# Gate-loop attention with a maxout FFN on one core: the attention output computed with features in rows, on four column quarters of the array

## The chip, the cores and the metric

The kernel runs on one core of a Trainium2 chip. The metric is the device time of one execution in microseconds (us), the smaller the better. PE is TensorE's matmuls, PEld its weight loads, DVE VectorE, ACT ScalarE, POOL GpSimd and SP SyncE.

## The reference

```python
# batch 4, heads 8, sequence 768, head dim 48; all float32
for t in range(S):                                   # complex gated recurrence, per head
    new_re = ar * S_re - ai * S_im                   # ar, ai: the normalised gate of token t
    new_im = ar * S_im + ai * S_re
    S_re, S_im = new_re + k_t (x) v_t, new_im
    y[:, :, t] = einsum('bhd,bhde->bhe', q_t, S_re)
x = y.transpose(0, 2, 1, 3).reshape(3072, 384)       # tokens x features
h = max(x @ w1, x @ w2, x @ w3)                      # 384 -> 768
out = h @ w_out                                      # 768 -> 384
```

The kernel turns the recurrence into blocks of 128 tokens (two chunks of 64). Within a chunk, every output is a sum over the chunk's tokens (a 64 x 64 matrix `atm` of scores per head, times V). What came earlier enters through a state G (the decayed query `QG`, times G).

## The kernel before

A group is two blocks. For each block TensorE makes transposes of K and Q (`tp`), decay sums (`mds`, `sfx`, `F`), scores (`A`, `B`), the state update (`dk`), and the output `y`. Between those blocks the FFN of the group before is woven in (`up`: 384 to 768, three weights; `op`: 768 to 384). `cs` is a running sum over tokens for the gates of the next group, and it waits for DVE's `w`. The FFN needs `x` with features in rows, while `y` comes out with tokens in rows, so y is copied out of PSUM, transposed by three PE transposes, and copied again.

```python
    vbs = [const.tile([P, H, 2, D], FP, name="vb%d" % i) for i in range(4)]
...
    def load_v(g):
        if g >= NG:
            return
        for c in range(C):
            x = g * C + c
            T["v", x] = vbs[x % 4]
            for h in range(2):
                nc.sync.dma_start(out=T["v", x][h * L64:(h + 1) * L64, :, h], in_=rows(v, g, c, h * L64, L64))
...
    def state(x):

        s = x % NS
        if s == 0:
            T["G", x] = st.tile([P, H, 2, D], FP, tag="G", name="G")
            nc.gpsimd.memset(T["G", x][0:DD, :, 0], 0.0)
        ps = psS.tile([P, 2, 512], FP, tag="s", name="dk")
        for h in range(H):
            nc.tensor.matmul(out=ps[0:DD, h // HU, h % HU * 96:h % HU * 96 + 96],
                             lhsT=T["Kt", x][:, h].rearrange("p u d -> p (u d)"),
                             rhs=T["v", x][:, h].rearrange("p c d -> p (c d)"), start=True, stop=True)
        dk = ps[0:DD, :, 0:HU * 96].rearrange("p a (b c d) -> p a b c d", b=HU, c=2)
        G = T["G", x]
        for c in range(2 if s < NS - 1 else 1):
            if c == 0:
                new = G[0:DD, :, 1]
            else:
                T["G", x + 1] = st.tile([P, H, 2, D], FP, tag="G", name="G")
                new = T["G", x + 1][0:DD, :, 0]
            add = new.rearrange("p (a b) d -> p a b d", b=HU)
            if s + c == 0:
                nc.vector.tensor_copy(out=add, in_=dk[:, :, :, c])
                continue
            f = T["F", x][0:DD, :, CD + c:CD + c + 1].to_broadcast([DD, H, D])
            nc.vector.tensor_tensor(out=new, in0=G[0:DD, :, c], in1=f, op=OP.mult)
            nc.vector.tensor_tensor(out=add, in0=add, in1=dk[:, :, :, c], op=OP.add)

    def outputs(x):
        atm, V, G, QG = T["atm", x], T["v", x], T["G", x], T["QG", x]
        y = psM.tile([P, DM], FP, tag="mm", padded_shape=[P, 512], name="y")
        for h in range(H):
            for new in (True, False):
                for c in range(2):
                    o = c * L64
                    nc.tensor.matmul(out=y[o:o + L64, h * D:(h + 1) * D],
                                     lhsT=atm[:, h] if new else QG[0:DD, 2 * h + c],
                                     rhs=V[:, h, c] if new else G[0:DD, h, c], start=new, stop=not new)
        T["x", x] = fp2.tile([P, DM], FP, tag="x", name="x")
        nc.scalar.copy(out=T["x", x], in_=y)

    def xt_step(x, xs):
        n = len(xs) * P
        if x == xs[0]:
            T["xT", xs[-1]] = fp2.tile([P, KD, n], FP, tag="xT", padded_shape=[P, KD, TG], name="xT")
        tp = psM.tile([P, KD, P], FP, tag="mm", padded_shape=[P, 4, P], name="tpx")
        for f in range(KD):
            nc.tensor.transpose(out=tp[:, f], in_=T["x", x][:, f * P:(f + 1) * P], identity=ident)
        o = (x - xs[0]) * P
        nc.scalar.copy(out=T["xT", xs[-1]][:, :, o:o + P], in_=tp)
...
    def up_step(xs, fp, i):
        xT, n = T["xT", xs[-1]], len(xs) * P
        ...  # up[f] += ws[i][:, d, f].T @ xT[:, d]: xT has features in rows
...
    def loop_steps(g):
        steps = []
        for x in range(g * C, (g + 1) * C):
            tr, ct, pr = front(x + 1)
            kt = [products(x + 1)[2]] if x + 1 < NX else []
            steps += [call(scores, x, "A"), call(gather, x, "A"), call(scores, x, "B")] + tr[:1]
            steps += [call(gather, x, "B"), call(state, x)] + tr[1:] + ct + pr[:1] + kt
            steps += [call(outputs, x)] + pr[1:2] + [call(xt_step, x, tokens(x))] + pr[2:]
        return steps
```

Of the kernel before, what the change touches and what calls it, by code (L numbers as in the profile page):

```python
# [9 lines left out]
FP = mybir.dt.float32  # L10
# [4 lines left out]
OP = mybir.AluOpType  # L15
# [30 lines left out]
def kernel(  # L46
# [13 lines left out]
    nc = tc.nc  # L60
    B, H, S, D = q.shape
    P = 128
# [26 lines left out]
    nat2 = ctx.enter_context(tc.tile_pool(name="nat2", bufs=2))  # L89
    un1 = ctx.enter_context(tc.tile_pool(name="un1", bufs=1))  # L90
    un2 = ctx.enter_context(tc.tile_pool(name="un2", bufs=2))
    st = ctx.enter_context(tc.tile_pool(name="st", bufs=2))
    fp2 = ctx.enter_context(tc.tile_pool(name="fp2", bufs=2))
    psS = ctx.enter_context(tc.tile_pool(name="psS", bufs=2, space=PSUM))
    psM = ctx.enter_context(tc.tile_pool(name="psM", bufs=4, space=PSUM))
# [49 lines left out]
    masko = const.tile([P, 4, 32], U8, name="masko")  # L145


    vbs = [const.tile([P, H, 2, D], FP, name="vb%d" % i) for i in range(4)]
    atms = [const.tile([P, H, L64], FP, name="atm%d" % i) for i in range(2)]

    def constants_early():
# [26 lines left out]
    def constants_late():  # L178
# [21 lines left out]
        for t in atms:  # L200
            nc.gpsimd.memset(t, 0.0)


    def rows(a, g, c, lo=0, n=P):
        b, s = divmod(g, GB)
        t0 = (s * C + c) * P + lo
        return a[b, :, t0:t0 + n, :].rearrange("h t d -> t h d")
# [15 lines left out]
# [4 lines that stand above are left out]
            x = g * C + c  # L227
            T["v", x] = vbs[x % 4]
            for h in range(2):
                nc.sync.dma_start(out=T["v", x][h * L64:(h + 1) * L64, :, h], in_=rows(v, g, c, h * L64, L64))  # L230

    ws = [const.tile([P, KD, FF], FP, name="w%d" % i) for i in range(3)]
    wo = const.tile([P, KF, DM], FP, name="wo")
# [270 lines left out]
    def state(x):  # L504

        s = x % NS
        if s == 0:
            T["G", x] = st.tile([P, H, 2, D], FP, tag="G", name="G")
            nc.gpsimd.memset(T["G", x][0:DD, :, 0], 0.0)
        ps = psS.tile([P, 2, 512], FP, tag="s", name="dk")  # L510
        for h in range(H):
            nc.tensor.matmul(out=ps[0:DD, h // HU, h % HU * 96:h % HU * 96 + 96],  # L512
                             lhsT=T["Kt", x][:, h].rearrange("p u d -> p (u d)"),
                             rhs=T["v", x][:, h].rearrange("p c d -> p (c d)"), start=True, stop=True)
        dk = ps[0:DD, :, 0:HU * 96].rearrange("p a (b c d) -> p a b c d", b=HU, c=2)
        G = T["G", x]
        for c in range(2 if s < NS - 1 else 1):
            if c == 0:
                new = G[0:DD, :, 1]
            else:  # L520
                T["G", x + 1] = st.tile([P, H, 2, D], FP, tag="G", name="G")
                new = T["G", x + 1][0:DD, :, 0]
            add = new.rearrange("p (a b) d -> p a b d", b=HU)
            if s + c == 0:
                nc.vector.tensor_copy(out=add, in_=dk[:, :, :, c])
                continue
            f = T["F", x][0:DD, :, CD + c:CD + c + 1].to_broadcast([DD, H, D])
            nc.vector.tensor_tensor(out=new, in0=G[0:DD, :, c], in1=f, op=OP.mult)
            nc.vector.tensor_tensor(out=add, in0=add, in1=dk[:, :, :, c], op=OP.add)  # L529

    def outputs(x):
        atm, V, G, QG = T["atm", x], T["v", x], T["G", x], T["QG", x]
        y = psM.tile([P, DM], FP, tag="mm", padded_shape=[P, 512], name="y")
        for h in range(H):
            for new in (True, False):
                for c in range(2):
                    o = c * L64
                    nc.tensor.matmul(out=y[o:o + L64, h * D:(h + 1) * D],  # L538
                                     lhsT=atm[:, h] if new else QG[0:DD, 2 * h + c],
                                     rhs=V[:, h, c] if new else G[0:DD, h, c], start=new, stop=not new)  # L540
        T["x", x] = fp2.tile([P, DM], FP, tag="x", name="x")
        nc.scalar.copy(out=T["x", x], in_=y)


    def xt_step(x, xs):
        n = len(xs) * P
        if x == xs[0]:
            T["xT", xs[-1]] = fp2.tile([P, KD, n], FP, tag="xT", padded_shape=[P, KD, TG], name="xT")
        tp = psM.tile([P, KD, P], FP, tag="mm", padded_shape=[P, 4, P], name="tpx")
        for f in range(KD):  # L550
            nc.tensor.transpose(out=tp[:, f], in_=T["x", x][:, f * P:(f + 1) * P], identity=ident)
        o = (x - xs[0]) * P
        nc.scalar.copy(out=T["xT", xs[-1]][:, :, o:o + P], in_=tp)  # L553

    def up_step(xs, fp, i):
        xT, n = T["xT", xs[-1]], len(xs) * P
# [24 lines left out]
    def call(f, *a):  # L581
        return lambda: f(*a)
# [21 lines left out]
# [4 lines that stand above are left out]
            kt = [products(x + 1)[2]] if x + 1 < NX else []  # L608
            steps += [call(scores, x, "A"), call(gather, x, "A"), call(scores, x, "B")] + tr[:1]
            steps += [call(gather, x, "B"), call(state, x)] + tr[1:] + ct + pr[:1] + kt  # L610
            steps += [call(outputs, x)] + pr[1:2] + [call(xt_step, x, tokens(x))] + pr[2:]
        return steps

    table("natural_log_exp_and_others")
    for t in vbs:
        nc.gpsimd.memset(t, 0.0)
    load(0)
    load_v(0)
# [54 lines left out]
```

## Time and profile before

| what | before |
|---|---|
| median of 3 timed executions | 777.61 us (777.31 to 778.47) |
| the profiled execution | 776.25 us, span 774.3 us, clock 0.969 |
| PE busy in the span | 698.6 us (90%) |
| DVE, ACT busy | 515.8 us (67%), 405.5 us (52%) |
| one group of two blocks, steady | 56.87 us, of which PE busy 56.45 |
| y, 32 matmuls = 64 records, of one block | 2.00 us |
| three transposes of one block, in the chain | 0.33 us |

The prediction shows the lines behind this table. A group in the chain of waits is the distance from one block to the same block two further on. A "record" is what the profile counts as one instruction: a float32 matmul of the code shows as two records, a transpose as one.

### The profile page before, as it was taken

The numbers are of one execution on the slowest core, as the hardware profiler recorded it, in microseconds if no ns is written. First come the engines' busy times: TensorE is split into PE (matmuls) and PEld (weight loads), VectorE is DVE, ScalarE is ACT, GpSimd is POOL, SyncE is SP. The second block draws the span as 40 slices with busy tenths as digits, with TensorE's granted clock in tenths as the row PEclk, the third lists the DMA queues.
The fourth block names the chain that finished last, engine by engine and source line by source line (L and its number), as shares of the span: only waits on it lengthen the run. The fifth ranks groups of instructions, "written<-read, shape, count | busy, mean of one in ns | idle before, by whom it ended". The sixth has DMA issues, their size and how long they took to land.

```text
span 774.3 us, 14595 instructions
## 1 busy us (share of the span) xinstructions
PE 698.6 (90%) x6156; PEld 570.3 (74%) x6156; DVE 515.8 (67%) x706; ACT 405.5 (52%) x677; POOL 115.9 (15%) x124
## 2 busy tenths in 40 slices
PE   1174579999799999999999999999999999999998
PEld 0063378978678778878878878878878878878775
DVE  4899997788764865865855856866766767645211
ACT  6685645667555564664564564564564564412010
POOL 7003100403102202202102112112112013000000
PEclk9987589999899999999999999999999999999999
DMA  9663430050220320410410410410410210000000
GB/s 228 108 175 115 119 82 23 11 103 2 52 62 11 63 52 11 77 38 11 83 40 4 85 40 2 93 31 7 87 32 12 42 32 2 1 21 2 11 11 20
DMA packets 133377, 38.70 MB, mean 50 GB/s; under 512 B 126016, under 2 KB 129088, under 8 KB 133312
## 3 DMA queue, kind: packets, MB, share of 16 engines
q1 hardware_dynamic: 133056, 37.76, 22.0%
q8 instruction: 48, 0.79, 0.4%
q14 instruction: 17, 0.14, 0.1%
q10 hardware_dynamic: 256, 0.01, 0.0%
HBM read 33.03 MB, written 4.72 MB: 49 GB/s over the span
## 4 chain that ended last, share of the span: by engine, by line
PE 70%; DVE 18%; ACT 2%; issue 1%; DVEq 0%; ACTq 0%
PE up L564 30%; PE op L575 12%; PE tp L416 5%; PE dk L512 4%; PE y L538 4%; PE F L433 4%; PE B L476 4%; DVE QB L443 3%; DVE Q L443 3%; PE cs L337 3%; PE A L476 2%; DVE QG L443 2%; DVE KB L443 2%; DVE w L333 1%; DVE w L334 1%; PE sfx L377 1%
## 5 line engine op out<-in xcount | busy, mean ns | idle before, releaser
L564 PE MATMUL up<-xT,w 128*128 128x256 f32 (+1 forms) x1404 | 301.3, 366 | 0.7 <-ACT xT L553 0.7
L564 PEld LDWEIGHTS up<-xT,w 128*128 128x128 f32 x1404 | 246.6, 191 | 38.1 <-issue 1.1
L569 DVE TENSOR_TENSOR hT<-hT,up 128x512 f32<-128x512 f32 (+1 forms) x78 | 50.1, 642 | 87.4 <-PE up L564 85.5
L575 PE MATMUL op<-wo,hT 128*128 128x384 f32 x288 | 98.1, 490 | 0.0
L316 POOL TENSOR_TENSOR ai<-ai,L 128x768 f32<-128x768 f32 x11 | 27.6, 2509 | 394.0 <-ACT L L107 361.5
L575 PEld LDWEIGHTS op<-wo,hT 128*128 128x128 f32 x288 | 52.9, 190 | 32.6
L419 ACT COPY K<-tp 96x512 f32<-96x512 f32 x48 | 27.9, 581 | 78.0 <-PE tp L416 77.8
L443 DVE TENSOR_TENSOR Q<-Q,F 96x512 f32<-96x512 f32 x48 | 41.7, 869 | 31.9 <-ACT F L107 31.9
L443 DVE TENSOR_TENSOR QB<-Q,F 96x512 f32<-96x512 f32 (+1 forms) x48 | 53.4, 1130 | 0.0
L538 PEld LDWEIGHTS y<-vb,atm 128*64 128x64 f32 x768 | 40.4, 141 | 12.7 <-issue 11.4
L538 PE MATMUL y<-vb,atm 128*64 128x48 f32 x768 | 48.6, 228 | 0.0
L538 PE MATMUL y<-G,QG 96*64 96x48 f32 x768 | 47.8, 226 | 0.0
L387 POOL TENSOR_TENSOR k<-E,k 128x384 f32<-128x384 f32 x22 | 28.9, 1316 | 125.3 <-ACT E L107 120.6
L476 PE MATMUL A<-Q,K 96*64 96x96 f32 x768 | 38.5, 254 | 10.2 <-DVE Q L443 10.2
L567 ACT COPY hT<-up 128x512 f32<-128x512 f32 (+1 forms) x39 | 21.3, 548 | 50.2 <-PE up L564 49.1
L337 PE MATMUL cs<-w,upto 128*128 128x384 f32 x48 | 22.5, 599 | 27.6 <-DVE w L334 27.6
L476 PEld LDWEIGHTS A<-Q,K 96*64 96x64 f32 x768 | 33.7, 140 | 18.3 <-DVE Q L443 10.9
L476 PE MATMUL B<-QB,KB 96*64 96x96 f32 x768 | 41.6, 254 | 3.3 <-DVE QB L443 3.3
L476 PEld LDWEIGHTS B<-QB,KB 96*64 96x64 f32 x768 | 35.9, 141 | 11.5 <-issue 4.0
L377 PE MATMUL mds<-Ln,mid 128*128 128x384 f32 x48 | 24.1, 587 | 19.8 <-DVE Ln L306 19.8
L538 PEld LDWEIGHTS y<-G,QG 96*64 96x64 f32 x768 | 40.6, 141 | 0.5 <-DVE G L529 0.5
L494 DVE COPY_PREDICATED atm<-masko,B 128x256 f32<-128x256 uint8 x72 | 31.6, 439 | 11.4 <-PE B L476 10.5
(106 smaller groups left out, 1156.8 us busy)
## 6 DMA issues: line engine op xcount, KB each, us to landing
ar<-in_a_re_dram SPq DMA_DIRECT2D x24, 192.0 KB, 3.7
ai<-in_a_im_dram SPq DMA_DIRECT2D x24, 192.0 KB, 3.8
k<-in_k_dram SPq DMA_DIRECT2D x24, 192.0 KB, 2.9
q<-in_q_dram SPq DMA_DIRECT2D x24, 192.0 KB, 3.3
vb<-in_v_dram SPq DMA_DIRECT2D x48, 96.0 KB, 3.0
raw<-in_moe_w_dram SPq DMA_DIRECT2D x6, 768.0 KB, 5.5
out_dram<-ot SPq DMA_DIRECT2D x24, 192.0 KB, 1.9
wo<-in_moe_w_dram SPq DMA_DIRECT2D x3, 768.0 KB, 6.5
```

Source lines behind the costliest of these rows:

```text
L337: nc.tensor.matmul(out=ps, lhsT=upto, rhs=w[:, c * DM:(c + 1) * DM], start=True, stop=c == 0)
L377: nc.tensor.matmul(out=ps, lhsT=mat, rhs=T["Ln", g][:, c * DM:(c + 1) * DM], start=True, stop=True)
L416: nc.tensor.transpose(out=tp[0:DD, j], in_=T["U" + nm, x][:, hg * HU + j].rearrange("p u d -> p (u d)"), identity=ident)
L433: nc.tensor.matmul(out=ps[0:DD, j], lhsT=T["L2", x][:, hg * HU + j].rearrange("p u d -> p (u d)"), rhs=cuts, start=True, stop=True)
L443: nc.vector.tensor_tensor(out=out, in0=in_, in1=f.to_broadcast([DD, H, 2 * n, 8]), op=OP.mult)
L476: nc.tensor.matmul(out=ps[o:o + L64, h // HU, h % HU * 96:h % HU * 96 + 96], lhsT=K[0:DD, h, o:o + L64], rhs=Q[0:DD, 2 * h + c], start=Tru ...
L494: nc.vector.copy_predicated(out=out, mask=m, data=data)
L512: nc.tensor.matmul(out=ps[0:DD, h // HU, h % HU * 96:h % HU * 96 + 96], lhsT=T["Kt", x][:, h].rearrange("p u d -> p (u d)"), rhs=T["v", x] ...
L538: nc.tensor.matmul(out=y[o:o + L64, h * D:(h + 1) * D], lhsT=atm[:, h] if new else QG[0:DD, 2 * h + c], rhs=V[:, h, c] if new else G[0:DD, ...
L564: nc.tensor.matmul(out=ps[:, j], lhsT=ws[i][:, d, f * P:(f + 1) * P], rhs=xT[:, d], start=(d == 0), stop=(d == KD - 1))
L569: nc.vector.tensor_tensor(out=dst, in0=dst, in1=ps, op=OP.max)
L575: nc.tensor.matmul(out=ps, lhsT=hT[:, f, o:o + P], rhs=wo[:, f], start=(f == 0), stop=(f == KF - 1))
```

## The change

The roles in y's matmuls are swapped. V and G become the stationary operand, cut into pieces of 32 features, and the scores and the decayed query become the moving operand, 64 tokens wide. Each piece needs 32 columns of the array, so four pieces can lie side by side on four column quarters. The product then has features in rows and can be copied directly into `xT`: the copy of y into `x` and the three transposes go. A head has 48 features, which 32 does not divide. Two heads therefore share 96 rows, of which the middle 32 belong half to one head and half to the other. V and G are stored in 128 columns for two heads instead of 96: the first head, 32 columns of zeros, the second head. The middle 32 rows are then the sum of two pieces, each half zeros, one of each head.

The core of the diff (left out: new buffers `gs`, their clearing at the start, `vbs` of 1024 instead of 768 columns, V loaded as even and odd heads apart, so 96 transfers of half the size):

```diff
+    def heads(view):
+        dims = [list(d) for d in view.ap]
+        return bass.AP(view.tensor, view.offset, dims[:-1] + [[P - D, 2], [1, D]])
...
     def state(x):
 
         s = x % NS
+        T["G", x] = gs[x % 2]
         if s == 0:
-            T["G", x] = st.tile([P, H, 2, D], FP, tag="G", name="G")
-            nc.gpsimd.memset(T["G", x][0:DD, :, 0], 0.0)
+            nc.gpsimd.memset(T["G", x][0:DD, 0], 0.0)
         ps = psS.tile([P, 2, 512], FP, tag="s", name="dk")
         for h in range(H):
+            o = h % 2 * (P - D)
             nc.tensor.matmul(out=ps[0:DD, h // HU, h % HU * 96:h % HU * 96 + 96],
                              lhsT=T["Kt", x][:, h].rearrange("p u d -> p (u d)"),
-                             rhs=T["v", x][:, h].rearrange("p c d -> p (c d)"), start=True, stop=True)
+                             rhs=T["v", x][:, :, h // 2, o:o + D], start=True, stop=True)
         dk = ps[0:DD, :, 0:HU * 96].rearrange("p a (b c d) -> p a b c d", b=HU, c=2)
         G = T["G", x]
         for c in range(2 if s < NS - 1 else 1):
-            if c == 0:
-                new = G[0:DD, :, 1]
-            else:
-                T["G", x + 1] = st.tile([P, H, 2, D], FP, tag="G", name="G")
-                new = T["G", x + 1][0:DD, :, 0]
-            add = new.rearrange("p (a b) d -> p a b d", b=HU)
+            new = heads(G[0:DD, 1] if c == 0 else gs[(x + 1) % 2][0:DD, 0])
             if s + c == 0:
-                nc.vector.tensor_copy(out=add, in_=dk[:, :, :, c])
+                nc.vector.tensor_copy(out=new, in_=dk[:, :, :, c])
                 continue
             f = T["F", x][0:DD, :, CD + c:CD + c + 1].to_broadcast([DD, H, D])
-            nc.vector.tensor_tensor(out=new, in0=G[0:DD, :, c], in1=f, op=OP.mult)
-            nc.vector.tensor_tensor(out=add, in0=add, in1=dk[:, :, :, c], op=OP.add)
-
-    def outputs(x):
+            nc.vector.tensor_tensor(out=new, in0=heads(G[0:DD, c]), in1=f, op=OP.mult)
+            nc.vector.tensor_tensor(out=new, in0=new, in1=dk[:, :, :, c], op=OP.add)
+
+    def outputs(x, xs):
+
         atm, V, G, QG = T["atm", x], T["v", x], T["G", x], T["QG", x]
-        y = psM.tile([P, DM], FP, tag="mm", padded_shape=[P, 512], name="y")
-        for h in range(H):
-            for new in (True, False):
-                for c in range(2):
-                    o = c * L64
-                    nc.tensor.matmul(out=y[o:o + L64, h * D:(h + 1) * D],
-                                     lhsT=atm[:, h] if new else QG[0:DD, 2 * h + c],
-                                     rhs=V[:, h, c] if new else G[0:DD, h, c], start=new, stop=not new)
-        T["x", x] = fp2.tile([P, DM], FP, tag="x", name="x")
-        nc.scalar.copy(out=T["x", x], in_=y)
-
-
-    def xt_step(x, xs):
-        n = len(xs) * P
+        y = psM.tile([P, KD, P], FP, tag="mm", padded_shape=[P, 4, P], name="y")
+        queues = [[] for _ in range(4)]
+        for r in range(DM // 32):
+            i, w = divmod(r, 3)
+            runs = ((0,), (1, 2), (3,))[w]
+            for c in range(2):
+                todo = [(n, new) for new in (True, False) for n in runs]
+                queues[r % 4] += [(r, c, i, n, new, (n, new) == todo[0], (n, new) == todo[-1]) for n, new in todo]
+        for todo in zip(*queues):
+            for r, c, i, n, new, start, stop in todo:
+                h, lo = 2 * i + n // 2, 32 * n
+                nc.tensor.matmul(out=y[32 * (r % 4):32 * (r % 4) + 32, r // 4, c * L64:(c + 1) * L64],
+                                 lhsT=V[:, c, i, lo:lo + 32] if new else G[0:DD, c, i, lo:lo + 32],
+                                 rhs=atm[:, h] if new else QG[0:DD, 2 * h + c], start=start, stop=stop)
         if x == xs[0]:
-            T["xT", xs[-1]] = fp2.tile([P, KD, n], FP, tag="xT", padded_shape=[P, KD, TG], name="xT")
-        tp = psM.tile([P, KD, P], FP, tag="mm", padded_shape=[P, 4, P], name="tpx")
-        for f in range(KD):
-            nc.tensor.transpose(out=tp[:, f], in_=T["x", x][:, f * P:(f + 1) * P], identity=ident)
+            T["xT", xs[-1]] = fp2.tile([P, KD, len(xs) * P], FP, tag="xT", padded_shape=[P, KD, TG], name="xT")
         o = (x - xs[0]) * P
-        nc.scalar.copy(out=T["xT", xs[-1]][:, :, o:o + P], in_=tp)
+        nc.scalar.copy(out=T["xT", xs[-1]][:, :, o:o + P], in_=y)
+
...
-            steps += [call(outputs, x)] + pr[1:2] + [call(xt_step, x, tokens(x))] + pr[2:]
+            steps += [call(outputs, x, tokens(x))] + pr[1:]
```

## The prediction

> **What bounds the kernel now.** I read three views in this order: the page's busy shares and slices, the table of busy time by window, and the chain that ended last in one repeated stretch. The page says that TensorE is by far the busiest engine.
>
> ```profile
> PE 698.6 (90%) x6156; PEld 570.3 (74%) x6156; DVE 515.8 (67%) x706; ACT 405.5 (52%) x677; POOL 115.9 (15%) x124
> ...
> PE   1174579999799999999999999999999999999998
> ...
> PEclk9987589999899999999999999999999999999999
> ```
>
> From the sixth slice on (some 110 us) PE is nearly always busy, at full clock from the fifteenth. The kernel works on 24 blocks of 128 tokens, two per group. One group repeats from the chain's y block at 280.70 us to the one at 337.58 us, so I asked for windows of that length:
>
> ```profile
> core 0: us, PE busy (x) PEld busy (x) DVE busy (x) ACT busy (x) POOL busy (x), PEclk, DMA share, GB/s
> ...
> 280.70:337.58 56.88, 56.45 (x507) 46.16 (x508) 39.30 (x53) 31.74 (x53) 9.47 (x6) 1.00 0.21 43
> 337.58:394.39 56.81, 56.44 (x506) 46.15 (x508) 38.21 (x51) 31.86 (x53) 8.88 (x6) 1.00 0.21 43
> ```
>
> PE is busy 56.45 of 56.88 us, DVE only 39: about 0.4 us of PE idle is all that is left in a group. A microsecond of PE time is therefore worth nearly a microsecond, while ACT or POOL time is worth nothing. The chain through the same stretch says where that is not quite so, and what each kind of matmul costs:
>
> ```profile
> 280.70 2.00 PE y L538 x64
> 282.70 4.07 PE op L575 x12
> 286.77 0.33 PE tpx L551 x3
> 287.10 3.87 PE op L575 x12
> 290.97 1.47 PE A L476 x32
> 292.44 2.79 PE up L564 x12
> ...
> 300.30 1.36 PE dk L512 x16
> 301.66 0.87 PE tp L416 x8
> 302.53 2.59 PE up L564 x12
> 305.12 1.35 PE F L433 x16
> ...
> 314.05 1.85 DVE QG L443
> ...
> 317.77 0.97 DVE w L334
> ...
> 318.88 1.53 PE cs L337 x4
> ```
>
> For the second block of a group the chain is PE alone. For the first it leaves PE at 306.5 us (F, its exponential, then DVE's Q, KB, QB, QG, w) and returns at 318.88. In those 12 us PE is also almost full, and loses only the 0.4 us ahead of cs. DVE and PE are balanced there: a gain on PE alone may turn into a wait for QG or w.
>
> **Unit costs, from that chain.** A matmul in the code is two records (768 y matmuls in the code, 24 x 32; 2 x 768 in the profile), a transpose is one. Moving operand: up streams 256 columns in 2.59/12 = 216 ns, so 0.84 ns a column and record; tp, 128 columns in 0.87/8 = 109 ns, agrees; dk, 96 in 85 ns, is close. Stationary operand: F (96 stationary, only 74 moving columns, 62 ns by the above) needs 84 ns, so a weight load costs some 0.88 ns a column. A and y do better than this because the two 64-token halves lie on two column halves of the array: A, 96 columns, should take 81 ns a record and takes 1.47/32 = 46; y, where the load of 64 columns should set 56 ns, takes 2.00/64 = 31. In the timeline four y records start every 0.117 us, 29 ns each. So two halves already run fully side by side, each bounded by the larger of load and stream.
>
> **What the Trainium skill says.** "TensorEngine Tiling (Array Packing)", section Tiling Modes, lists 128x32 as four tiles, which load and multiply independently; its section Performance Considerations warns that a free dimension under about 60 columns gains nothing further. The trace shows the two-tile case only (31 against 56 ns); nothing in it uses four. "TensorE: Matmul & The Clock Gate", section LDWEIGHTS, makes the load proportional to stationary columns, columns/1.2 ns: 80 ns for F, measured 84. The same page, Part 3, says that loads overlap running matmuls only when the row group differs, and that matmuls are strictly first in, first out. Here the trace speaks against the first: both halves use all rows, and y would not reach 31 ns if their loads were serial. If some form of the second holds, it hurts the new form: in the built program the two records of one matmul stand next to each other on the same quarter.
>
> **The change part by part.**
> Removed: three transposes per block. In the chain they are 0.33 us; 24 x 0.33 = 7.9 us of PE. Also one ACT copy x<-y of 0.48 us per block (11.5 us of an engine at 52%: free), and the wait y, copy, transpose, copy, up. That wait is covered by other PE work except at the very end, where y ends at 735.0, the op fills until 738.4, and the transposes and the second copy hold up the last up stretch until 739.4: about 1 us gained once.
>
> Changed: y. Each block had 32 matmuls (64 stationary, 48 moving); now it has 64 (features as 32 stationary columns, 64 tokens moving): twice as many because 48 features are cut into 32-column pieces, the middle one shared by two heads. 64 records become 128. One record on a quarter: load 32 x 0.88 = 28 ns, stream 64 x 0.84 = 54 ns, so the stream sets about 56 ns with a small gap. With four quarters side by side, 128/4 x 56 = 1.8 us against 1.9 to 2.0 us now. So the new y is expected to cost what the old did, perhaps 0.1 us less. The wider quarters only pay for the doubled count: the gain is the transposes.
>
> Moved, read from the order of the built program: a group has the same blocks as before in nearly the same order; all of B now stands ahead of cs (before, 7 of 16 stood after), and QG comes one DVE instruction earlier. Between F and cs PE has mds 0.65, up 2.59, sfx 0.65, y 1.9, mds 0.65, up 2.59, A 1.47, B 1.47 = 12.0 us, against the DVE chain of 12.3. So cs still waits for some 0.3 us, but with the whole of B done.
>
> Added: V loads as twice as many transfers of half the size (96 of 48 KB), same 192-byte pieces, loaded a group ahead: no wait on V was in the profile. At the start POOL clears 6 buffers of 1024 columns instead of 4 of 768. The four took 2.76 us; I estimate 5.5, so the masks come 2.8 us later. The first mds waited for the last mask until 11.8 us, but its exponential ran at 19.9 us, so that is hidden; DVE waited 2 us on a mask at 15.7 us, and the built order puts mask copies later. I charge 0.5 us.
>
> Sum: a group 2 x (0.33 + 0.08) = 0.8 us, perhaps 0.1 of the idle 0.4 more: 56.9 becomes some 56.0. Some 10 saturated groups, from 166 us to 735 us: -9 us. The two groups before, where DVE converts weights and the chain is only partly PE: -1. End: -1. Start: +0.5. Total about -10.5 us, so 777.6 becomes 767.
>
> **Rivals.**
> 1. Only two quarters overlap (in-order issue of the two records on one quarter, a limit of issue, or of the reading of four moving operands at once). Then y is 128/2 x 56 = 3.6 us, +1.6 a block, +38 - 10 = +28 us: 806. For it: y now never issues closer than one load and one matmul per 29 ns on average, and the new form needs 14 ns; nothing in the trace proves that rate. Against: the starts of the two halves' records lie some 7 ns apart and A runs at its stream limit, so the issue has room, and the skill lists the mode. I give something of this kind 1 in 4; a partial form (2.5 us a y) would give some 780.
> 2. DVE becomes the bound between F and cs: QG cannot be written before y has read the old QG (one buffer), and w follows. For it: the balance above. Against: y ends 1.6 us before QG starts now. If half of the gain falls there, only the second block's 0.4 us per group remain: about 772.
> 3. The gain is larger because the removed buffers and copies free PSUM slots earlier and the PE idle of 0.4 us goes altogether: another 10 x 0.3 = -3, about 763. Little speaks for it, as QG and w come when they come.
>
> **Range and chances.** The first account and rivals 2 and 3 fill 763 to 773, with some three chances in four. Rival 1 in part or in full fills 775 to 808. Hence 767, 80% between 761 and 791. Faster by over 2% means under 762.1, which the removed PE time does not hold: 0.06. Slower by over 2% means over 793.2, most of rival 1 in full: 0.13. Within 2%: 0.81.
>
> **What would show it.** y as x128 of about 1.8 to 1.9 us in the chain (rival 1: over 3); 128 y records per block, 3072 in all; no tpx, no x copy; a group of about 56.0 us with PE busy some 55.6; the copy into xT still 0.48 us; PE waiting at A or cs for QG or w by a few tenths at most. A y over 2.3 us, or a group length that stays at 56.8 although y and the transposes are as computed, would make the prediction wrong: the first in the unit cost on quarters, the second in the balance with DVE.

## More of the kernel before

The steady part of the kernel is nearly all PE. The first 240 us are not: there PE is busy for only 175 us, while DVE is busy for 190 and ACT for 153 us, with the conversion of the weights among other things.

## The result, and the profile after

The changed kernel took 768.39 us (median of 4 executions, 767.42 to 769.91), beside 777.46 us for the kernel before (median of 4, 777.19 to 778.47). The ratio is 0.9883, with a 95% interval of 0.9861 to 0.9905. Here and below, a ratio is the mean time of one kernel's fast runs over that of the other's of the same rounds, so it is not quite the ratio of the medians quoted. The gain is 9.1 us, 1.2%. That is within 2%, 1.4 us above the predicted 767 and inside the range of 761 to 791.

The page's busy shares and slices after, to set beside the three lines that the prediction shows:

```profile
PE 686.5 (89%) x7620; PEld 559.8 (73%) x7620; DVE 514.8 (67%) x706; ACT 393.5 (51%) x653; POOL 126.1 (16%) x126
...
PE   1264479999799999999999999999999999999998
...
PEclk9987588999999999999999999999999999999999
```

PE has more instructions (the y records have doubled, the transposes have gone) and 12.1 us less busy time. ACT lost its 24 copies: 12.0 us less. The shape over time is the same: PE is nearly always busy from the seventh slice on (116 us; the prediction says the sixth, which reads 7 tenths in both). The two rows of y in the page's table of groups count the records (columns: line, engine, operation, names, shapes of the stationary operand and the moving one, count; then busy time and the mean of one):

```profile
L550 PE MATMUL y<-atm,vb 128*32 128x64 f32 x1536 | 46.2, 222 | 0.0
L550 PE MATMUL y<-QG,g 96*32 96x64 f32 x1536 | 45.6, 220 | 0.0
```

These are 3072 records, as predicted. The 222 ns is the duration of one record from start to end, and records overlap, so it is not what a record costs; that is read from the chain. Here is the chain that ended last, through one steady stretch after (start, duration, what, how many records):

```profile
341.28 1.95 PE y L550 x118
...
361.45 1.35 PE F L442 x16
...
370.38 1.78 DVE QG L452
372.25 0.67 DVE hT L573
372.92 1.08 DVE w L342
374.65 0.85 DVE w L343
375.63 1.53 PE cs L346 x4
```

There are three readings. First, y costs 1.95 us where it was 2.00: the doubled count of records is paid for by the four quarters (r_pairs and r_seq below show that they run side by side). (The chain lists 118 of the block's 128 records; another stretch shows 126. The duration is the same.) Second, there is no tpx any more. Third, the DVE part from F to cs has become longer: F starts at 361.45 and cs at 375.63, while the first w starts at 372.92 and the second ends only at 375.50, although the two last 1.93 us together. In between stands another DVE instruction of 0.65 us, a predicated copy of scores into `atm`, which nothing on this path needs. From the end of F to cs there are 12.83 us. Before, the two w followed each other directly, and the prediction's lines give 12.41 (306.47 to 318.88). Less the wait at its end (0.75 and 0.43 us in the timeline), PE has 12.1 and 12.0 us of work in this stretch, so nearly all of the added 0.42 us is idle PE. Busy time by window, from one cs to the next:

```profile
core 0: us, PE busy (x) PEld busy (x) DVE busy (x) ACT busy (x) POOL busy (x), PEclk, DMA share, GB/s
...
319.71:375.63 55.92, 55.17 (x626) 45.20 (x627) 39.22 (x53) 30.83 (x51) 9.06 (x6) 1.00 0.22 44
375.63:431.80 56.17, 55.40 (x627) 45.18 (x627) 37.85 (x50) 30.76 (x51) 9.53 (x6) 1.00 0.22 44
```

A group now takes 56.1 us on average, with PE busy 55.3. PE's idle time per group grew from 0.4 to nearly 0.8 us.

PE busy fell by 1.1 us a group, more than the transposes and y explain. The rest is B, of which the page's rows are, before and after:

```profile
L476 PE MATMUL B<-QB,KB 96*64 96x96 f32 x768 | 41.6, 254 | 3.3 <-DVE QB L443 3.3
```

```profile
L485 PE MATMUL B<-QB,KB 96*64 96x96 f32 x768 | 38.5, 254 | 3.3 <-DVE QB L452 3.3
```

The B work is the same, but before, cs cut it in two in each group (18 records ahead of cs, 14 behind, with an `up` stretch between); after, it is whole. The next table adds up the timeline by kind of block, each from its start to the start of the next one, in us per group, as the mean of the seven steady groups that the table further down marks. Idle PE is the group less PE's busy time and is taken out of the blocks. The last three columns are experiments told below.

| us per group | before | after | r_tpx | r_btune | r_tune3 |
|---|---|---|---|---|---|
| six transposes | 0.75 | 0 | 0.75 | 0.65 | 0 |
| two B | 3.26 | 2.96 | 3.26 | 2.89 | 2.89 |
| two y | 4.01 | 3.89 | 3.89 | 4.00 | 3.89 |
| all other PE work | 48.42 | 48.47 | 48.43 | 48.71 | 48.73 |
| idle PE | 0.42 | 0.77 | 0.49 | 0.35 | 0.35 |
| group | 56.86 | 56.09 | 56.82 | 56.60 | 55.86 |

So the change takes 0.75 us of transposes, 0.30 of B and 0.12 of y out of a group, and adds 0.35 of idle PE.

What PE waits for, between 320 and 700 us (total, times, longest), before:

```profile
PE cs L337 <- DVE w L334: 2.5, 6, 0.4
```

and after:

```profile
PE cs L346 <- DVE w L343: 5.3, 7, 0.8
```

The window holds six of these waits before and seven after, so it is 0.42 us each time before and 0.76 after.

The end of the kernel, in the chain before:

```profile
733.10 1.88 PE y L538 x58
734.98 3.44 PE op L575 x10
...
738.48 0.31 ACT ot L577
...
738.86 0.49 ACT xT L553
...
739.39 2.64 PE up L564 x11
```

and after:

```profile
730.16 1.99 PE y L550 x125
...
732.17 0.49 ACT xT L556
...
732.70 2.42 PE up L568 x10
```

Before, from the end of the last filler (op, 738.42) to the last up stretch (739.39) there are 0.97 us, and some 0.3 of them are the transposes. After, from the end of y (732.15) to up there are 0.55. (After, the scheduler ran the op matmuls before y.)

To see where the time went, I use the seventh and the 21st dk block in the trace as marks. Between them lie seven steady groups. The table has the profiled executions only; "after again" and "before again" are second profiles of the same files (r_after, r_null), the other two are experiments told below.

| profile | to the 7th dk | seven groups | PE busy in them | to the end | span |
|---|---|---|---|---|---|
| before | 243.2 | 398.1 | 395.2 | 133.0 | 774.3 |
| before again | 244.4 | 398.1 | | 132.9 | 775.4 |
| after | 244.4 | 392.6 | 387.2 | 130.6 | 767.6 |
| after again | 244.0 | 392.7 | | 130.5 | 767.2 |
| r_tpx | 246.0 | 397.7 | 394.3 | 131.8 | 775.5 |
| r_bstart | 246.1 | 398.1 | | 133.0 | 777.1 |

The steady part gains 5.5 us and the part behind it 2.4. Ahead of it, the two profiles of either kernel cannot tell the two apart: means of 243.8 and 244.2, with 1.2 us between two executions of the same file. The profiled execution of before was also one of its quickest (776.25 us, where its timed ones lie between 776.2 and 779.1), so the difference of the spans, 6.7 us, understates the gain of 9.1 that the medians show. Of these 9.1 us, 7.9 are located (5.5 and 2.4); the other 1.2 are not.

### The profile page after: what moved, and what is told of

It is laid out like the page before. It is cut to its first block, busy times and chain, and to the rows that moved or that the text cites. A ratio compares the mean times of both kernels' runs of the same rounds, so it can differ in the third digit from the quotient of the medians.

```text
span 767.6 us, 17622 instructions
## 1 busy us (share of the span) xinstructions
PE 686.5 (89%) x7620; PEld 559.8 (73%) x7620; DVE 514.8 (67%) x706; ACT 393.5 (51%) x653; POOL 126.1 (16%) x126
## 4 chain that ended last, share of the span: by engine, by line
PE 66%; DVE 20%; issue 7%; ACT 3%; POOL 2%; SPq 1%; DMA 1%; POOLq 0%; DVEq 0%; ACTq 0%
PE up L568 29%; PE op L579 12%; PE tp L425 5%; PE dk L522 4%; DVE QB L452 4%; PE F L442 3%; DVE Q L452 3%; PE y L550 3%; PE cs L346 3%; PE B L485 2%; DVE QG L452 2%; PE A L485 2%; DVE KB L452 2%; DVE w L342 2%; DVE Kt L410 1%
## 5 line engine op out<-in xcount | busy, mean ns | idle before, releaser
L568 PEld LDWEIGHTS up<-xT,w 128*128 128x128 f32 x1404 | 249.4, 192 | 38.9 <-issue 1.0
L325 POOL TENSOR_TENSOR ai<-ai,L 128x768 f32<-128x768 f32 x11 | 30.8, 2795 | 374.6 <-ACT L L106 223.0
L452 DVE TENSOR_TENSOR Q<-Q,F 96x512 f32<-96x512 f32 x48 | 43.3, 902 | 17.7 <-ACT F L106 17.7
L346 PE MATMUL cs<-w,upto 128*128 128x384 f32 x48 | 22.5, 599 | 35.3 <-DVE w L343 30.3
L550 PEld LDWEIGHTS y<-atm,vb 128*32 128x32 f32 x1536 | 38.9, 110 | 12.6 <-issue 11.8
L106 ACT ACTIVATE F<-F 96x296 f32<-96x296 f32 x48 | 19.6, 412 | 54.6 <-PE F L442 54.1
L550 PE MATMUL y<-atm,vb 128*32 128x64 f32 x1536 | 46.2, 222 | 0.0
L550 PE MATMUL y<-QG,g 96*32 96x64 f32 x1536 | 45.6, 220 | 0.0
L485 PE MATMUL B<-QB,KB 96*64 96x96 f32 x768 | 38.5, 254 | 3.3 <-DVE QB L452 3.3
L346 PEld LDWEIGHTS cs<-w,upto 128*128 128x128 f32 x48 | 9.6, 223 | 42.9 <-DVE w L343 20.3
L442 PEld LDWEIGHTS F<-cuts,L 128*96 128x96 f32 x384 | 38.4, 169 | 3.2 <-ACT L L438 1.7
```

The source lines that it names most:

```text
L325: (nc.gpsimd if g > 0 else nc.vector).tensor_tensor(out=ai, in0=ai, in1=L, op=OP.mult)
L346: nc.tensor.matmul(out=ps, lhsT=upto, rhs=w[:, c * DM:(c + 1) * DM], start=True, stop=c == 0)
L442: nc.tensor.matmul(out=ps[0:DD, j], lhsT=T["L2", x][:, hg * HU + j].rearrange("p u d -> p (u d)"), rhs=cuts, start=True, stop=True)
L452: nc.vector.tensor_tensor(out=out, in0=in_, in1=f.to_broadcast([DD, H, 2 * n, 8]), op=OP.mult)
L485: nc.tensor.matmul(out=ps[o:o + L64, h // HU, h % HU * 96:h % HU * 96 + 96], lhsT=K[0:DD, h, o:o + L64], rhs=Q[0:DD, 2 * h + c], start=Tru ...
L550: nc.tensor.matmul(out=y[32 * (r % 4):32 * (r % 4) + 32, r // 4, c * L64:(c + 1) * L64], lhsT=V[:, c, i, lo:lo + 32] if new else G[0:DD, c ...
```

## The experiments

All of them gave correct results, and all were compared with the kernel before on the same chip.

### r_after: the changed kernel again

No edit.

> The changed kernel unaltered, beside the others on the same chip: ratio to the kernel before 0.986 to 0.991, a group of 56.1 us between two cs blocks, PE idle in it 0.75 us, y x128 in 1.95 us.

Measured: 768.53 us (767.57 to 769.85), ratio 0.9886 [0.9867, 0.9906], beside 777.2 us before. It repeats the first result. A difference under some 1.5 us between two kernels is within what one execution differs from the next.

### r_tpx: the transposes and their copy put back

```diff
+    def extra(x, xs):
+        o = (x - xs[0]) * P
+        tp = psM.tile([P, KD, P], FP, tag="mm", padded_shape=[P, 4, P], name="tpx")
+        for f in range(KD):
+            nc.tensor.transpose(out=tp[:, f], in_=T["xT", xs[-1]][:, f, o:o + P], identity=ident)
+        sink = fp2.tile([P, KD, P], FP, tag="x", name="sink")
+        nc.scalar.copy(out=sink, in_=tp)
-            steps += [call(outputs, x, tokens(x))] + pr[1:]
+            steps += [call(outputs, x, tokens(x))] + pr[1:2] + [call(extra, x, tokens(x))] + pr[2:]
```

The sink is never read: this adds the cost of the removed steps to the changed kernel without their use.

> The transposes and a second copy are put back behind the new y (their result is used by nothing; outputs stay right). Theory (the gain is the PE time of the transposes): two times 0.33 us of PE a group come back; the built order between F and cs is again that of the kernel before. A group of 56.6 to 56.8 us, PE busy 56.0 to 56.3, time 774 to 778 (ratio 0.995 to 1.000). Rival (the gain came from the new order or from y itself, and the transposes lie in waits): a group of 56.1 to 56.3, time within 3 us of the changed kernel, 767 to 771.

Measured: 776.5 us (775.45 to 777.19), ratio to before 0.9988 [0.9973, 1.0003]: the whole gain is gone but for some 0.7 us. Its chain has the new y and the old transposes, and B cut in two again by cs (these are the 14 records behind it):

```profile
383.12 0.81 PE B L485 x14
...
397.06 1.95 PE y L550 x124
...
403.07 0.33 PE tpx L562 x3
```

The cost is 8.0 us beside r_after, where 24 x 0.33 = 7.9 was expected. That they agree so closely is partly luck, because two effects of the order nearly cancel. PE busy time in the seven groups is 7.1 us more for 14 blocks, 1.0 us a group. By the table of blocks above, 0.75 us of it are the transposes and 0.30 us B, which cs cuts in two as in the kernel before. But the groups are only 5.1 us longer, 0.73 each, because the wait at cs shrinks (3.4 us in seven waits between 320 and 700 us, against 5.3 in seven). The built order of this kernel between F and cs is that of before again, with no copy between the two w. So removing the transposes gives the gain and, through the scheduler, also moves the order on PE (B whole, a gain) and on DVE (the copy between the two w, a loss). The copy into the sink comes back with the transposes; on PE's account it does not show.

### r_pairs and r_seq: fewer quarters side by side

```diff
-        for todo in zip(*queues):
+        for todo in list(zip(*queues[:2])) + list(zip(*queues[2:])):   # r_pairs
+        for todo in queues:                                            # r_seq
```

The same 128 records of a block, with the same operands; only the order in which they are issued differs.

> Same 64 matmuls of y a block, but issued so that only two quarters alternate at a time: first quarters 0 and 1, then 2 and 3. Theory (four quarters run side by side, each bounded by its stream of 64 columns, 56 ns): two side by side need 128/2 x 56 = 3.6 us a y instead of 1.95, 1.65 us more a block, total 768 + 24 x 1.65 = 806 to 810. Rival (TensorE looks far enough ahead, or y is bounded by something that does not depend on the number of quarters, such as issue): y stays at 1.9 to 2.3 us, total under 778.

> Same matmuls, one quarter after the other. Theory: nothing runs side by side but at the three changes of quarter; a y takes up to 128 x 56 ns = 7.2 us, total 768 + 24 x 5.2 = 890 or a little less. Rival (look-ahead): the more TensorE reaches past the queue of one quarter, the shorter y; at a full look-ahead 2 us and 770.

Measured: 801.87 us with two quarters in turn and 870.12 us with one after the other. The y rows of the chain, r_pairs and then r_seq:

```profile
378.68 3.55 PE y L550 x128
```

```profile
371.83 6.75 PE y L550 x128
```

So y is 1.95, 3.55 and 6.75 us on four, two and one quarter at a time, that is 61, 55 and 53 ns for each set of records that can run together (32, 64 and 128 sets). In r_seq, records on one quarter follow each other at the streaming time of 64 columns (64 x 0.84 = 54 ns); records on different quarters overlap in these three orders only as far as they stand next to each other in the program. The first rival of the prediction (y at 3.6 us, 806 us in all) is thus what this kernel would have been without the interleaving. It comes to 802 and not 806 partly because the group grew by 2.9 us (59.0 from 56.1) and not by 2 x 1.6 = 3.2: with more PE work before it, cs waits less (3.1 us in seven waits between 320 and 700 us, against 5.3). Both totals missed what was expected of them, 806 to 810 and some 890 us, on the low side, the second also because y took 6.75 us and not 7.2.

### r_gather: the copy between the two w moved behind them

```diff
+        T["w2"] = nc.vector.tensor_tensor(out=w[:, lo:hi], in0=w[:, lo:hi], in1=ai[:, lo:hi], op=OP.add)
...
+            ins = nc.vector.copy_predicated(out=out, mask=m, data=data)
+            if x % C == C - 1:
+                tc.add_manual_dep(ins.ins, T["w2"].ins.name, order, reason="gather after w")
```

The added dependency is one of order on the same engine; no wait is taken away.

> One ordering constraint on DVE, without a wait: for the second block of a group the first copies of the scores come after the product chain w that cs needs, as in the kernel before, instead of between its two instructions. Theory (in the changed kernel PE idles 0.75 us a group before cs because DVE is 0.65 us later with w): idle before cs falls to 0.1 to 0.4 us, a group takes 55.6 to 55.8 us, total 763.5 to 766 (ratio 0.982 to 0.985). Rival (DVE is the bound over the whole group, so what is not lost before cs is lost later): the group stays at 56.0 to 56.1, total within 1.5 us of the changed kernel.

Measured: 768.3 us (767.71 to 770.38), ratio 0.9888 [0.987, 0.9906]: no change, so the expectation was missed. The DVE stretch did become shorter: from F's last record to cs there are 12.35 us (360.75 to 373.10) instead of 12.83. But the scheduler, with other times to go by, put only 12 of the 16 B matmuls ahead of cs, so PE had less to do while it waited, and most of the wait stayed (0.63 us each time, against 0.76):

```profile
PE cs L346 <- DVE w L343: 3.8, 6, 0.7
```

What the shorter wait gave went back into PE busy time: 388.6 us in the seven groups, against 387.2, with B cut in two by cs again. The group stayed at 56.2 us. A shorter DVE chain is only worth something here if PE keeps its fill of work ahead of cs.

### r_start, r_mask and r_bstart: the start

r_start spreads the clearing: two V buffers on POOL, two on DVE, the G buffers later with `atms`. r_mask makes DVE's four mask copies follow the second w of the first group. r_bstart goes the other way: it is the kernel before with both costs that the change adds at the start, V loaded as 96 half transfers, and POOL clearing 6144 columns instead of 3072.

```diff
# r_start
-        for t in atms:
+        for t in atms + gs:
-    for t in vbs + gs:
+    for t in vbs[:2]:
         nc.gpsimd.memset(t, 0.0)
+    for t in vbs[2:]:
+        nc.vector.memset(t, 0.0)
# r_mask (T["w2"] as in r_gather)
+                ins = nc.vector.tensor_copy(out=dst[o:o + L64], in_=f[o:o + L64, :, o // L64])
+                tc.add_manual_dep(ins.ins, T["w2"].ins.name, order, reason="masks after w")
# r_bstart, in the kernel before
+                src = rows(v, g, c, h * L64, L64).rearrange("t (i u) d -> t i u d", u=2)
+                for u in range(2):
+                    dst = T["v", x][h * L64:(h + 1) * L64, :, h].rearrange("p (i u) d -> p i u d", u=2)
+                    nc.sync.dma_start(out=dst[:, :, u], in_=src[:, :, u])
+    spare = const.tile([P, 4 * 256 + 2 * 1024], FP, name="spare")
+    for o in range(0, 3072, 1024):
+        nc.gpsimd.memset(spare[:, o:o + 1024], 0.0)      # after the four V buffers
```

> Only the clearing of buffers at the start is moved: two V buffers stay first on POOL, two go to DVE while it waits for the first loads, the two state buffers are cleared after the masks. Theory (the first 160 us lost some 3 us because POOL makes the masks 2.6 us later, and DVE waits 1.25 and 1.44 us for them): DVE no longer waits over 0.5 us for a mask, the first cs comes at 33.5 us or before (34.5 now), and the total falls by 1 to 3 us (ratio 0.984 to 0.987). Rival (the loss of the start is made later, by the order in which the scheduler places y, up and the weights' conversion between 90 and 160 us): first cs earlier, but the cs of the third group still at 160 us or later, total unchanged within 1 us.

> As the changed kernel, but the copies of the masks on DVE are ordered (without a wait) behind the chain w of the first group, so DVE does not wait for POOL's masks while the first chain is open. Theory (the later masks cost the start 1 us or more): no wait of DVE for a mask, first cs at 33.5 us or earlier (34.4), total 766.5 to 767.8 (ratio 0.985 to 0.988). Rival (DVE is full with the weights' conversion until 110 us, so an earlier first cs is lost again there): first cs earlier, total 768 to 769.5.

> The kernel before with both costs that the change adds at the start and nothing else of it: V loads as twice as many transfers of half the size (heads of even and odd number apart), and POOL clearing as many columns as the changed kernel (three unused pieces of 1024 columns after the four V buffers). Theory A (these two make the changed kernel some 3 us late at the third cs): third and fourth cs about 3 us later than before's 157.7 and 202.9 us, and 779.5 to 781 us in all. Theory B (the lateness comes from the new order of instructions in the first two groups, or is scatter of single profiles): within 1 us of before, 776.5 to 778.5 us, the first cs up to 1 us later.

Measured: r_start 769.21 us (768.51 to 770.48), ratio 0.9897 [0.9882, 0.9912]; r_mask 767.84 us (767.15 to 768.37), ratio 0.9872 [0.9857, 0.9887]; r_bstart 777.78 us (776.71 to 778.85), ratio to before 0.9995 [0.9983, 1.0008] in five rounds.

r_start missed: its first cs came at 35.3 us, not earlier than the 34.5 of the changed kernel. With the clearing spread, the scheduler put the mask copies earlier, and DVE waited for POOL's masks longer than in the changed kernel (there 1.3 and 1.4 us). What DVE waits for in its first 40 us:

```profile
DVE maskd L183 <- POOL maskf L120: 2.3, 1, 2.3
...
DVE masko L183 <- POOL maskf L120: 1.6, 1, 1.6
```

In r_mask the first cs does come early, at 31.9 us (although one wait for a mask, of 1.7 us, stays), but the third is at 159.6, against 160.9 in the changed kernel and 157.7 before: half of what is gained at the start is lost by then. Its total lies between the two forecasts and within noise of the changed kernel, so it decides nothing. r_bstart settles what the two start costs are worth: nothing that five rounds can show (at most 0.0008 of 777 us, 0.6 us), as its theory B said. Its profile, of its slowest execution, had the third cs at 159.8 us and the seventh dk at 246.1, late by 2 to 3 us as its theory A said, while its times are those of before. So a few microseconds' difference of single profiles over the first 240 us is no evidence for a cause. Before r_bstart I had read the changed kernel as starting some 3 us late (third cs 160.9 against 157.7), and planned r_start and r_mask on that reading.

### r_null: the kernel before, profiled again

No edit.

> The kernel before, unaltered, profiled a second time. Its first profile was of a quick execution (776.25 us where the others lie between 776.2 and 779.1) and had its seventh dk block at 243.2 us; the old-order kernels r_tpx and r_bstart had it at 246.0 and 246.1, the changed kernel at 244.4 and 244.0. Theory (the changed kernel's late start was the scatter of that one profile): the seventh dk block here lies between 244.5 and 247 us and the span between 775 and 777.5. Rival (the old start is really 2 to 3 us quicker): 243.2 again, within 0.6. From the seventh to the 23rd dk block 457.6 us as before in either case; ratio 1 within 0.2%.

Measured: 777.6 us (777.24 to 777.75), ratio 1.0001 [0.9984, 1.0018], span 775.4 us, the seventh dk at 244.4 us. That lies just below what the theory allowed and outside what the rival allowed (243.2 within 0.6). Two profiles of one file differ by 1.2 us there; the seven groups agree to 0.1 us. What the change did to the first 240 us is therefore not settled below 1 to 2 us.

### r_tune2, r_tune3 and r_btune: the order set by hand, with and without the change

r_tune2 joins the edits of r_gather and r_mask to the changed kernel and fixes three more places: both score products stand before the first gather, cs follows the last B matmul, and the last three steps of the next group's preparation (the gate angles with cs, and the two products behind them) have fixed places in the loop. r_tune3 is the same file again. r_btune is the kernel before with exactly these edits. (`T["scored"]` is the last score matmul issued; the lines that keep it, and the edits shown above, are left out.)

```diff
+            ins = nc.tensor.matmul(out=ps, lhsT=upto, rhs=w[:, c * DM:(c + 1) * DM], start=True, stop=c == 0)
+            if g > 1 and c == 0:
+                tc.add_manual_dep(ins.ins, T["scored"].ins.name, order, reason="cs after B")
...
-            steps += [call(scores, x, "A"), call(gather, x, "A"), call(scores, x, "B")] + tr[:1]
+            steps += [call(scores, x, "A"), call(scores, x, "B"), call(gather, x, "A")] + tr[:1]
...
-            weave((0.0, 1.0, loop_steps(g)), (0.0, 0.7, pre_steps(g + 1)), (0.0, 1.0 if g > 1 else 0.5, ffn_steps(xs)))
+            pre = pre_steps(g + 1)
+            late = [(0.56, 0.56, pre[5:6]), (0.6, 0.6, pre[6:7]), (0.656, 0.656, pre[7:8])] if pre else []
+            weave((0.0, 1.0, loop_steps(g)), (0.0, 0.4375, pre[:5]), *late, (0.0, 1.0 if g > 1 else 0.5, ffn_steps(xs)))
```

> The masks as in the run above, and the group reordered by ordering constraints alone: the copies of the second block's scores come after w on DVE, and on TensorE all of A and B and, by the built order, one more up stretch come before cs, so 2.6 us more PE work stands between F and cs. Theory (the changed kernel loses 0.75 us a group to the wait of cs for w, and only filling PE ahead of cs takes it away): no wait at cs, a group of 55.3 to 55.6 us, total 761 to 764 (ratio 0.979 to 0.983). Rival (the wait moves behind cs: the next transposes wait for Uk, which comes out of cs): PE waits at tp instead, a group of 55.8 to 56.2, total 766 to 769.

> The kernel before (with the transposes) with exactly the edits of order that r_tune2 made to the changed kernel. Theory: those edits only take away waits that both kernels have or the scheduler's disorder, and the transposes still cost 0.33 us a block and stand on the TensorE path; so a group of two blocks stays at PE busy 56.45 us, the idle ahead of cs (0.4 us) goes, the group is 56.4 to 56.6 us, and the time is 770 to 774 us, with 8 to 10 us more than the tuned changed kernel of the same rounds. Rival: the room that the tuning uses exists only without the transposes (their wait y, copy, transpose, copy, up then sits in the way), so the old kernel gains under 2 us: 775.5 or more. Second rival: the tuning gains the same 7 us here, 770 or less.

> The same file as r_tune2, once more beside the two others, so that the tuned changed kernel and the tuned old one have the same chip: 760 to 762.5 us again, groups of 55.5 to 56 us; if the verdict of faster by over 2% was luck, the ratio here lies above 0.982.

Measured: r_tune2 761.44 us (760.3 to 761.65), ratio 0.9785 [0.9769, 0.9802]; r_tune3 761.83 us (760.31 to 762.0), ratio 0.9791 [0.9776, 0.9806]; r_btune 769.15 us (768.47 to 771.62), ratio 0.989 [0.9872, 0.9907], beside 778.56 us before. The tuned changed kernel is faster than both kernels. Against the one before the mean gain is 2.1% in both calls, but both intervals reach just past 0.98, so by over 2% is not shown: the verdict is unclear, and the expectation for r_tune3 spoke too soon of "the verdict of faster by over 2%". All that PE waits for by over half a microsecond in total in its steady part (r_tune3, 320 to 700 us) is now this:

```profile
PE tp L428 <- DVE Uk L404: 1.1, 5, 0.2
PE tp L428 <- DVE Uq L404: 0.9, 4, 0.2
```

The wait at cs is gone. A group takes 55.9 us (391.1 us for seven) with PE busy 55.5. So r_tune2's total fell where its theory put it (761 to 764), and its group where the rival did (55.8 to 56.2), with the short waits of tp for Uk that the rival named. In r_btune it takes 56.6 us (396.2 for seven): the wait at cs goes there too, and the transposes stay. So the ordering is not a gift of the change. It is worth 9.4 us to the old kernel and 6.7 us to the new one (r_tune3 against the 768.5 of r_after), and between the two tuned kernels the change is worth 7.3 us. These two have the same order, B whole in both and the same idle time, so they show the change by itself: in the table of blocks they differ in the transposes (0.65 us a group) and y (0.11), and in all other PE work together by 0.02. My expectation for r_btune was right on the group and wrong on the total: the second rival, 770 or less, holds. The larger part of what ordering gains lies before the steady part: the seventh dk is at 238.4 us in r_btune and 237.4 in r_tune3, some 5 to 7 us earlier than in the untuned kernels. Which of the five edits does that was not taken apart; r_mask, which has one of them, did not.

## Why the prediction was right, and where its steps were off

The result lies 1.4 us from the predicted 767 and inside the range, in the likeliest class. Step by step:

1. **The bound.** "A microsecond of PE time is therefore worth nearly a microsecond" held roughly: r_tpx, which puts back the transposes and their copy, gives back 8.0 us, where the prediction worked out 7.9 for them. r_pairs and r_seq add PE time and pay for 87 and 88% of it (33 of 24 x 1.6 = 38 us, 102 of 24 x 4.8 = 115 us).
2. **The y block.** Four quarters side by side was right, and the unit cost was some 8% short: 1.95 us measured, "1.8 us against 1.9 to 2.0" predicted. Of the saving of 0.08 us a block about 0.05 is there. With 53 ns a record from r_seq, 32 sets make 1.7 us; the further 0.25 us is what the interleaved form loses, on which no run says more.
3. **The removed transposes, and B.** The transposes were nearly right: 0.75 us a group, and 0.65 with the order set by hand, where 2 x 0.33 was predicted. But PE busy in a group fell by 1.1 us to 55.3, where 55.6 was predicted. The largest part of the difference is B, which cs no longer cuts in two (0.30 us). The prediction had read this order from the built program ("all of B now stands ahead of cs") and used it for the wait alone; it gave it no value in PE time.
4. **The wait at cs.** "PE waiting at A or cs for QG or w by a few tenths at most", 0.3 us expected: mis-sized. It measured up to 0.8 us, 0.35 more than before. The stretch from F to cs is 0.42 us longer, with nearly the same PE work in it, and what is new on DVE there is the copy of scores between the two w. This is the second rival in part (DVE between F and cs), by a way that the prediction had not named: not QG waiting for y, but DVE's own order. r_tpx shows the order going back with the transposes, and the tuned pair shows the wait can be ordered away; r_gather moved the copy alone, but B moved with it, so no run isolates the copy. The longer wait cancels the unpriced gain of B in point 3: a group fell by 0.8 us (56.9 to 56.1), where 0.9 was predicted. That the group came out so near is in part luck: two effects of the order that the prediction had not priced happen to be of nearly one size. The mechanism that it had priced, transposes and y, is shown alone by the tuned pair: 0.65 and 0.11 us, 0.74 a group in all, where 2 x (0.33 + 0.08) = 0.8 was predicted.
5. **The end.** "About 1 us gained once" was too much: the gap ahead of the last up stretch went from 0.97 to 0.55 us, of which some 0.3 was the transposes that were counted already.
6. **The start.** "+0.5" and "-1" for the first groups cannot be checked at this size. r_bstart shows that the added transfers and clearing cost at most 0.6 us together (the upper end of its interval); the profiles scatter by 1.2 us.
7. **ACT's copy.** Free, as said: ACT lost 12.0 us of busy time, and nothing in the waits of PE answers to it.

The first rival was real but did not come: r_pairs shows 801.9 us for it. The third (763 by larger gains) did not come in the change itself, though the tuned order shows that even less than 763 (761.8) was there to be had, in another way than this rival's.

What stays open: what the change does to the first 240 us below 1 to 2 us, and with it 1.2 us of the gain; which ordering edit gains the 5 to 7 us there; and what the copy between the two w costs by itself.

## What to carry to other kernels

If a product has to be transposed only so that the next product can use it, try swapping stationary and moving operands. Here, with narrow stationary pieces side by side on parts of the array, the swap cost nothing even at twice the instruction count (1.95 us against 2.00), but only with the pieces interleaved in program order (6.75 us without). Count the gain from the removed PE work on the path, then read the chain again for what the scheduler did with the order of every engine, PE too: here it gave 0.30 us a group on PE and took back 0.35 in the wait for DVE, and setting the order by hand was worth about as much as the change (6.7 to 9.4 us, against 7.3 to 9.1). Do not explain a difference of one or two microseconds between single profiles before the unchanged kernel has been profiled twice.

## What the Trainium skill lacked or had wrong

- "TensorE: Matmul & The Clock Gate", Part 3, says in its list of what overlaps that weight loads overlap running matmuls only when the row group differs (its text above the list also allows a load into a background weight buffer, so the two do not agree). Here all tiles use the same 128 (or 96) rows and differ in columns only, and loads and matmuls of four quarters overlap: y takes 1.95 us interleaved and 6.75 us one quarter after another, for the same 128 records. Even on a single quarter the load hides: 6.75/128 = 53 ns a record is the streaming time of 64 columns alone (0.84 ns each, 54 ns), with nothing left for the load of 32. So the list is too narrow.
- The same part's table of measured speedups has column packing of three tiles at 512 moving columns (2.38 times). It has no case of four column tiles alone and none with few moving columns. This case gives four tiles at 64 columns: 3.46 times over one tile at a time (6.75/1.95) and 1.82 times over two (3.55/1.95).
- "TensorEngine Tiling (Array Packing)", Tiling Modes, says that tiles work in parallel but not that the order of issue decides it. r_pairs and r_seq issue the same instructions as the changed kernel in another order and lose the overlap, 3.55 and 6.75 us against 1.95. This agrees with the strict first in, first out of matmuls that "TensorE: Matmul & The Clock Gate", Part 3, states; neither page draws the consequence.
- "FP8 and Floating Point Precision", TensorE Precision Notes, gives true float32 as four passes through the array. The profile shows two records for each float32 matmul, of 0.84 ns a moving column each; no page read tells how passes and records relate, which one needs for counting.
